# A staging pool of its own for w_out in the second product, two pairs' sums made in the first, and first w_in tiles loaded two steps sooner

## The chip, the cores and the metric

The kernel runs on one core of a Trainium2 chip. The metric is the device time of one execution in microseconds. The engines are TensorE (PE, with its weight loads as PEld), VectorE (DVE), ScalarE (ACT), GpSimd (POOL) and SyncE (SP), whose queue issues nearly all transfers.

## The reference

Attention over 8 sequences of 448 tokens with 12 heads of 64, with a sigmoid in place of the softmax, and then a feed-forward block on its 3584 x 768 output, all in float32:

```python
scores = scale * np.matmul(q, k.transpose(0, 1, 3, 2)) - np.log(S)
attn = 1.0 / (1.0 + np.exp(-scores))
x = np.matmul(attn, v) ...            # (3584, 768)
h = x @ w_in                          # (768, 2048)
relu6 = np.clip(h + 3.0, 0.0, 6.0)
g = h * relu6 / 6.0
return (g @ w_out).astype(np.float32) # (2048, 768)
```

Both weights come as float64, and the kernel turns them into float32 on the chip ("decode").

## The kernel before, in words

**Three stages.** The attention takes 168 steps of scores and attention-times-v, and 2 more. The first product (x @ w_in) is made of 7 products M1 to M7 per block (Strassen in Winograd's form), for 16 blocks q = 0 to 15, four for each of the four pairs of sequences p: 112 slots, one product of 18 matmuls in each, in the order of `slots()`. The second product (g @ w_out) has the same seven products, in the order M1, M2, M6, M7, M5, M4, M3. Five of them run over the four pairs, two units of 36 matmuls each; M6 and M3 are cut once more ("fine") and run over couples of pairs (c = 0 and 1). In all stages a float32 operand is split into a rounded part (a cast on ACT) and the rest (a subtraction on DVE), and three matmuls stand for one.

**Names.** `ws` is a w_in tile that has been loaded, `w` its split form; a slot's tile is loaded 5 slots ahead and split 3 and 2 slots ahead. `g` is the first product's output, stored to DRAM as `gd`; `gr` is such a tile read back and `gx` its split form, one for each unit of the second product (`gx_0` to `gx_7` are those of M1, `gx_8` to `gx_15` those of M2). `wo` is a raw w_out tile, decoded into `w2`; `w2s` a w_out tile read back from DRAM (`dw2`) for a product, whose split form is again `w`. `td` holds, in DRAM, the sums of g over two pairs that M6 and M3 need.

**What sets the order.** The program is written out in order for every engine, and each engine runs its own list from top to bottom. A table by slot (`at_slot`), by unit (`at_fetch`, `at_unit`, `at_end`) or by attention step (`on`, `on_late`) says at which place a piece of work is written. SP's list is one of these: a transfer that waits holds up all behind it. Each transfer also waits for the one eight places ahead of it, since eight semaphores go round.

**Staging.** Raw w_out tiles, w_in tiles and `w2s` tiles share one tag with three buffers. In the second product nine raw w_out tiles (e = 0 to 8) are loaded two units ahead of the unit in which their decode begins; one raw tile's decode is one instruction on ACT (line 66) and six on DVE (lines 68 to 79).

**Sums over two pairs.** For M6 they are made in the first product while the second of the two pairs is at work: `twin_load` reads the first pair's tile back, `twin_sums` makes four subtractions and additions of 128 x 448 on DVE, `twin_store` writes two tiles of 448 KB. For M3 they are made in the second product: `pre_load` (four loads of 448 KB), `pre_sums` (four operations of 128 x 896), `pre_store` (four stores), twice for each c; for c = 0 this starts at units 3 and 6, in M1.

The lines that set these places before:

```python
for n in range(LA):                                  # LA = 3
    on(NS - (12, 11, 8)[n], w1_load, n)
    over(on, (NS - (8, 5, 4)[n],), gen)              # cast on ACT
    over(on_late, (NS - (7, 4, 3)[n],), gen)         # rest on DVE
...
for c, n in enumerate((3, begin[M7] + 1)):
    for r in range(2):
        at_fetch(n + 3 * r, pre_load, c, r)
        at_end(n + 3 * r + 1, pre_sums)
        at_fetch(n + 3 * r + 2, pre_store, c, r)
```

Of the kernel before, what the change touches and what calls it, by code (L numbers as in the profile page):

```python
# [108 lines left out]
def tile_kernel(ctx: ExitStack, tc: tile.TileContext, qk, vP, wi, wo, outT):  # L109
# [42 lines left out]
    def staging(name, shape, dtype):  # L152
        return dw.tile(shape, dtype, tag="stg", name=name, bufs=3)
# [4 lines left out]
    def temp(tag, bufs, name, shape=(P, 2, S)):  # L158
        return tmp.tile(list(shape), F32, tag=tag, name=name, bufs=bufs)
# [9 lines left out]
    def on(s, f, *a):  # L169
        events.setdefault(s, []).append((f, a))  # L170
# [4 lines left out]
    def at_slot(n, f, *a):  # L175
        later.setdefault(n, []).append((f, a))
# [4 lines left out]
    def at_fetch(n, f, *a):  # L181
        fetch.setdefault(n, []).append((f, a))

    def at_end(n, f, *a):
        finish.setdefault(n, []).append((f, a))

    def over(when, steps, gen):
        for n in steps:
            when(n, next, gen, None)
# [104 lines left out]
            nc.sync.dma_start(out=dw1[q][:, :4, r], in_=a)  # L294
            nc.sync.dma_start(out=dw1[q][:, 4:, r], in_=s)

    def w2_unit(k, h, ec, held):

        st = staging(f"wo_{k}_{h}_{ec}", [P, FC * P, 2], I32)
        nc.sync.dma_start(out=st, in_=wo[k, h, :, ec * FC * P : (ec + 1) * FC * P])  # L300
        yield
        if ec == 0:
            held[k, h] = ring(f"w2_{k}_{h}", [P, EC, FC * P], F32)
        yield from decode(nc, st, held[k, h][:, ec])
        if ec == EC - 1 and (k, h) in ((A11, 0), (A12, 0), (A11, 1)):
# [164 lines left out]
    def twin_load(q):  # L470
        p, j = divmod(q, NQ)
        quad[q, "twin"] = temp("v", 3, f"twin_{q}")
        nc.sync.dma_start(out=quad[q, "twin"], in_=gd[p - 1, T2][:, :, j])

    def twin_sums(q):
        b1, b2 = quad[q, "twin"], quad[q, T2]
        t = quad[q, "diff"] = temp("T", 3, f"diff_{q}")
# [5 lines left out]
    def twin_store(q):
        p, j = divmod(q, NQ)
        for k, t in enumerate(("diff", "twin")):
            nc.sync.dma_start(out=td[M6, p // 2, k][:, :, j], in_=quad[q, t])
# [6 lines left out]
    def post(i, q, n):  # L493
        if i == M1:
            copied(q, "s1")
        elif i == M6:
            copied(q, "u2")
            if q // NQ % 2:
                at_slot(n + 2, twin_load, q)
        elif i == M7:  # L500
            copied(q, "u3")
            if ("D", q) in acc:
                at_slot(n + 1, c22, q, n + 1)
        elif i == M5:
# [212 lines left out]
    def w2_direct(i, h):  # L717
        w2s[i, h] = made[h].pop(WEIGHT[i])

    for e in range(3 * EC):  # L720
        k, ec = divmod(e, EC)
        gen = w2_unit((A12, A21, A22)[k], 1, ec, held)
        at_fetch(e - 2, next, gen, None)
        over(at_unit, [e, e + 1, e + 1, e + 1, e + 1], gen)
    at_unit(4, w2_keep, A12, 1)
# [27 lines left out]
        keep["up"] = stack.enter_context(tc.tile_pool(name="up", bufs=1, side="right", reuse_waits="tile"))  # L753
        return stack

    for c, n in enumerate((3, begin[M7] + 1)):
        at_fetch(n, swap, None, (), "pre", pre_open)
        for r in range(2):
            at_fetch(n + 3 * r, pre_load, c, r)
            at_end(n + 3 * r + 1, pre_sums)  # L760
            at_fetch(n + 3 * r + 2, pre_store, c, r)
        at_fetch(n + 6, swap, "pre", (), None, None)
# [201 lines left out]
```

## Time and profile before

| what | value |
|---|---|
| median of 3 runs | 1077.87 us (1077.75 to 1077.89) |
| the profiled execution's own time | 1080.59 us |
| its span, first to last instruction | 1078.8 us |
| mean granted TensorE clock, as a share of 2.4 GHz | 0.992 |
| PE busy | 1059.8 us, 98% |
| DVE busy | 808.0 us, 75% |
| ACT busy | 584.6 us, 54% |
| transfers read and written | 209.58 MB and 100.79 MB |

An engine's busy time is the sum of its instructions' time. The span leaves out 1.79 us of the profiled execution (1080.59 - 1078.8); the median of the three runs, made without a profile, is 2.72 us below that execution. A wait costs the kernel time only where it holds up PE, the engine that is busy nearly all along.

### The profile page before, as it was taken

Reading aid. Unit: us, or ns where it says so; the run is one execution under the profiler, and the core shown is the slowest. Engines: PE = TensorE matmul, PEld = TensorE weight load, DVE = VectorE, ACT = ScalarE, POOL = GpSimd, SP = SyncE. Lnnn points to the kernel's source line nnn. Section 1 sums busy time; section 2 is a strip of 40 time slices with the busy share of each in tenths; the row PEclk is TensorE's granted clock in tenths of the full one; section 3 lists DMA queues with packets and bytes.
Section 4 is the critical chain, followed back from the end, with each engine's and each line's share of the span. In section 5 each row is a group of like instructions: output and inputs, shape, how many; then the busy total and the mean of one; then the engine's idle time right before and its main releaser. Section 6 shows DMA issues by size and latency. Waiting matters only on the chain.

```text
span 1078.8 us, 16857 instructions
## 1 busy us (share of the span) xinstructions
PE 1059.8 (98%) x6728; PEld 934.0 (87%) x6728; DVE 808.0 (75%) x862; ACT 584.6 (54%) x630; POOL 41.3 (4%) x39
## 2 busy tenths in 40 slices
PE   9999999999999999999999999987999999999998
PEld 6777777776999999999999998976999999999997
DVE  3879886773578878897787777867787669787684
ACT  7889988886446644664565555333344423232441
POOL 0314230000000000000000000000000000000000
PEclk9999999999999999999999999997999999999999
DMA  8887999885867888798676898878988589899392
GB/s 320 301 310 283 380 353 331 287 298 218 283 222 224 263 315 278 275 309 304 207 232 220 294 360 305 320 284 321 338 328 286 187 322 378 328 339 348 129 395 75
DMA packets 106591, 311.50 MB, mean 289 GB/s; under 512 B 9104, under 2 KB 54416, under 8 KB 106512
## 3 DMA queue, kind: packets, MB, share of 16 engines
q1 hardware_dynamic: 106368, 310.30, 80.9%
q8 instruction: 53, 0.87, 0.3%
q14 instruction: 26, 0.21, 0.1%
q10 hardware_dynamic: 144, 0.11, 0.0%
HBM read 209.58 MB, written 100.79 MB: 288 GB/s over the span
## 4 chain that ended last, share of the span: by engine, by line
PE 93%; DMA 3%; DVE 3%; issue 0%; ACT 0%; SPq 0%; DVEq 0%; ACTq 0%
PE po L861 24%; PE A L431 21%; PE sc L221 11%; PE pv L238 11%; PE D L431 10%; PE B L431 5%; PE m_A L861 4%; PE m_E L861 4%; PE m_D L861 2%; DMA ws<-dw 1%; PE m_B L861 1%; DMA w2s<-dw 1%; DMA pre<-gd 1%; DMA gr<-gd 1%; DVE gx L87 1%
## 5 line engine op out<-in xcount | busy, mean ns | idle before, releaser
L861 PE MATMUL po<-gx,w 128*128 128x448 f32 x1440 | 294.2, 366 | 11.5 <-ACT w L85 6.9
L861 PEld LDWEIGHTS po<-gx,w 128*128 128x128 f32 x1440 | 273.7, 190 | 31.6 <-ACT w L85 7.2
L431 PE MATMUL A<-x,w 128*128 128x448 f32 x1152 | 235.8, 362 | 0.0
L431 PEld LDWEIGHTS A<-x,w 128*128 128x128 f32 x1152 | 215.9, 188 | 15.1 <-issue 0.7
L85 ACT CAST gx<-gr 128x1792 fp32r<-128x1792 f32 x68 | 115.0, 1696 | 169.1 <-PE po L861 106.0
L221 PE MATMUL sc<-qk 64*64 64x448 f32 x1344 | 189.1, 538 | 1.6 <-ACT a L223 1.6
L223 ACT ACTIVATE a<-sc,bias_s 128x896 f32<-128x896 f32 x168 | 168.3, 1011 | 37.9 <-PE sc L221 34.9
L238 PE MATMUL pv<-a,v 64*64 64x448 f32 x1344 | 188.6, 536 | 0.0
L87 DVE TENSOR_TENSOR gx<-gr,gx 128x1792 fp32r<-128x1792 f32 x68 | 137.3, 2022 | 30.6 <-ACT gx L85 30.6
L221 PEld LDWEIGHTS sc<-qk 64*64 64x64 f32 x1344 | 89.5, 134 | 39.0 <-ACT a L223 5.8
L238 PEld LDWEIGHTS pv<-a,v 64*64 64x64 f32 x1344 | 91.4, 133 | 35.0 <-issue 2.5
L431 PE MATMUL D<-x,w 128*128 128x448 f32 x576 | 120.4, 362 | 1.3 <-DVE cD L460 1.3
L87 DVE TENSOR_TENSOR w<-ws,w 128x768 fp32r<-128x768 f32 x112 | 106.3, 953 | 13.7 <-ACT w L85 12.5
L431 PEld LDWEIGHTS D<-x,w 128*128 128x128 f32 x576 | 107.9, 188 | 8.8 <-issue 1.6
L85 ACT CAST w<-ws 128x768 fp32r<-128x768 f32 x112 | 93.1, 831 | 28.6 <-DMA ws<-dw 28.5
L249 DVE TENSOR_TENSOR xr<-pv,y 128x448 f32<-128x448 f32 x48 | 29.9, 623 | 61.0 <-ACT y L248 60.8
L431 PE MATMUL B<-x,w 128*128 128x448 f32 x288 | 60.2, 362 | 0.0
L431 PEld LDWEIGHTS B<-x,w 128*128 128x128 f32 x288 | 54.0, 187 | 3.6
L451 ACT ACTIVATE g<-cD,bias 128x896 f32<-128x896 f32 x32 | 33.5, 1047 | 40.9 <-DVE cD L460 40.9
L456 ACT COPY u<-A 128x896 f32<-128x896 f32 x32 | 29.0, 907 | 48.0 <-PE A L431 48.0
L85 ACT CAST w<-w2s 128x512 fp32r<-128x512 f32 x39 | 23.1, 618 | 55.7 <-DMA w2s<-dw 33.5
L460 DVE TENSOR_TENSOR cD<-D,u 128x896 f32<-128x896 f32 x32 | 34.8, 1089 | 21.1 <-ACT u L456 13.7
(94 smaller groups left out, 945.0 us busy)
## 6 DMA issues: line engine op xcount, KB each, us to landing
gr<-gd SPq DMA_DIRECT2D x52, 896.0 KB, 6.7
ws<-dw SPq DMA_DIRECT2D x112, 384.0 KB, 4.4
gd<-g SPq DMA_DIRECT2D x64, 448.0 KB, 5.0
qk<-qk SPq DMA_DIRECT2D x47, 448.0 KB, 5.9
gd<-gT SPq DMA_DIRECT2D x32, 448.0 KB, 6.0
gr<-td SPq DMA_DIRECT2D x16, 896.0 KB, 9.0
gr<-gd SPq DMA_DIRECT2D x32, 448.0 KB, 6.3
wi<-wi SPq DMA_DIRECT2D x16, 768.0 KB, 7.9
```

Of the source, the lines that this page charges most:

```text
L85: nc.scalar.copy(hi, a)
L87: nc.vector.tensor_tensor(out=lo, in0=a, in1=hi.bitcast(F32), op=ALU.subtract)
L221: nc.tensor.matmul(out, k[halves[r], at_k], q[halves[r]], start=True, stop=True)
L223: nc.scalar.activation(a, sc[:, :, :S], AF.Sigmoid, bias=bias_s, scale=scale)
L238: nc.tensor.matmul(pv[p][halves[j], r, :S], v, a[halves[r], int(r != j) if c is None else j], start=first, stop=last)
L249: nc.vector.tensor_tensor(out=xr[b, u][:, k], in0=pv[p][:, 1, :S], in1=y, op=ALU.add)
L431: nc.tensor.matmul(t[:, j, :S], w[:, wk, j, kc], x[:, xk, kc], start=i in (M1, M2, M5) and m == 0, stop=m == 3 * KC - 1, skip_group_check= ...
L451: nc.scalar.activation(r, h, AF.Relu, bias=bias_3, scale=1.0)
L456: nc.scalar.copy(acc[key, q], acc["A", q][:, :, :S])
L460: nc.vector.tensor_tensor(out=c, in0=acc[name, q][:, :, :S], in1=acc[key, q], op=ALU.add)
L861: nc.tensor.matmul(out, w[:, wk, c], x[:, xk, c], start=first and c == 0 and xk == 0 and wk == 0, stop=last and c == FC - 1 and wk == 1, s ...
```

## The change

It has four parts.

1. The first three w_in tiles are loaded 2, 2 and 1 attention steps sooner, and their splits are made 1, 0 and 1 steps later.
2. `w2_unit` takes the function that gives it a staging buffer. In the second product the tiles e = 3 to 8 get theirs from a pool `wo` of their own with three buffers, open from unit 1 to 5 units ahead of M6. The tiles e = 0 to 2 keep the shared tag.
3. M3's sums for c = 0 (the first two pairs) are made in the first product, with `twin_load`, `twin_sums` and `twin_store`, at 5, 8 and 10 slots after M3 of the blocks q = 7 to 10. Their `pre_load`, `pre_sums` and `pre_store` in the second product are gone. For this case both tiles are read back, the second into a buffer of tag `T` (`mate`).
4. The M6 sums of block q = 14 are made 4 slots later.

```diff
-    def w2_unit(k, h, ec, held):
+    def w2_unit(k, h, ec, held, stage=staging):
...
-        st = staging(f"wo_{k}_{h}_{ec}", [P, FC * P, 2], I32)
+        st = stage(f"wo_{k}_{h}_{ec}", [P, FC * P, 2], I32)
...
-        on(NS - (12, 11, 8)[n], w1_load, n)
+        on(NS - (14, 13, 9)[n], w1_load, n)
         gen = w1_split(n)
-        over(on, (NS - (8, 5, 4)[n],), gen)
-        over(on_late, (NS - (7, 4, 3)[n],), gen)
+        over(on, (NS - (7, 5, 3)[n],), gen)
+        over(on_late, (NS - (6, 4, 2)[n],), gen)
...
+    def twin_load(i, c, j, k, mate=None):
+        b1 = temp("v", 3, f"twin_{i}_{c}_{j}")
+        nc.sync.dma_start(out=b1, in_=gd[2 * c, k][:, :, j])
+        if mate is None:
+            mate = temp("T", 3, f"mate_{i}_{c}_{j}")
+            nc.sync.dma_start(out=mate, in_=gd[2 * c + 1, k][:, :, j])
...
             if q // NQ % 2:
-                at_slot(n + 3, twin_sums, q)
-                at_slot(n + 5, twin_store, q)
+                twin, held_up = (M6, q // NQ // 2, q % NQ), 4 * (q == NPR * NQ - 2)
+                at_slot(n + 3 + held_up, twin_sums, *twin, (q, T2))
+                at_slot(n + 5 + held_up, twin_store, *twin)
+            if 0 <= q - 2 * NQ + 1 < NQ:
+                twin = M3, 0, q - 2 * NQ + 1
+                at_slot(n + 5, twin_load, *twin, B22)
+                at_slot(n + 8, twin_sums, *twin)
+                at_slot(n + 10, twin_store, *twin)
...
+    at_fetch(1, w2_open)
+    at_fetch(begin[M6] - 5, w2_pool.close)
...
-        gen = w2_unit((A12, A21, A22)[k], 1, ec, held)
+        gen = w2_unit((A12, A21, A22)[k], 1, ec, held, staging if e < 3 else w2_stage)
...
-    for c, n in enumerate((3, begin[M7] + 1)):
...
+    n = begin[M7] + 1
```

**SP's list at the end of the attention**, before. `qk` and `v` are the attention's last inputs, `ws_0` to `ws_2` the first w_in tiles, `dw2` the stores of decoded w_out tiles.

```order
L198 DMA qk_46_2562<-qk 128x896
L203 DMA v_46_2564<-vP 128x896
L198 DMA qk_47_2610<-qk 128x896
L335 DMA dw2_4_0_79<-w2S1_0_2339 128x1536
L335 DMA dw2_5_0_81<-w2_0_0_2274 128x1536
L352 DMA ws_0_2637<-dw1_0_69 128x768
L352 DMA ws_1_2653<-dw1_0_69 128x768
L313 DMA dw2_1_0_75<-w2_1_0_2463 128x1536
L352 DMA ws_2_2695<-dw1_0_69 128x768
```

The same place in the change:

```order
L198 DMA qk_46_2562<-qk 128x896
L203 DMA v_46_2564<-vP 128x896
L352 DMA ws_0_2604<-dw1_0_69 128x768
L198 DMA qk_47_2612<-qk 128x896
L352 DMA ws_1_2621<-dw1_0_69 128x768
L335 DMA dw2_4_0_79<-w2S1_0_2339 128x1536
L335 DMA dw2_5_0_81<-w2_0_0_2274 128x1536
L352 DMA ws_2_2677<-dw1_0_69 128x768
L313 DMA dw2_1_0_75<-w2_1_0_2463 128x1536
```

The first two tiles now stand ahead of the two stores, and the third ahead of one.

**DVE's list where the first product ends**, before. `gx_0` to `gx_2` are the splits of the second product's first units, the `diff` and `twin` rows are M6's sums of blocks 14 and 15, `cD_15` is the sum for which the last M3 product waits, `gT` the last sums of `g`.

```order
L87 TENSOR_TENSOR gx_0_6047<-gr_0_5990,gx_0_6047 128x1792 [waits DMAHW1_49,Activation_49]
L478 TENSOR_TENSOR diff_14_6086<-gT2_14_6051 128x448 [waits DMAHW5_49,DVE_49]
L479 TENSOR_TENSOR diff_14_6086<-gT2_14_6051,twin_14_5872 128x448
L480 TENSOR_TENSOR twin_14_5872<-diff_14_6086,twin_14_5872 128x448 [waits DVE_49]
L481 TENSOR_TENSOR twin_14_5872<-twin_14_5872 128x448 [waits DVE_49]
L442 SCALAR_TENSOR_TENSOR g0_15_6074<-g0_15_6074,cB_15_6072 128x896 [waits Activation_49]
L460 TENSOR_TENSOR cD_15_6111<-D_15_6092,u3_15_6042 128x896 [waits PE_49]
```

The same list in the change, from `gx_1` on. Its rows from `gx_0` to `cD_15` read as before without the four rows of block 14.

```order
L87 TENSOR_TENSOR gx_1_6216<-gr_1_6127,gx_1_6216 128x1792 [waits DMAHW6_49,Activation_49]
L442 SCALAR_TENSOR_TENSOR g7_15_6199<-g7_15_6199,cD_15_6197 128x896 [waits DMAHW2_49,DVE_49]
L484 TENSOR_TENSOR diff_5_1_2_6221<-gT2_14_6095 128x448 [waits DMAHW5_49]
L485 TENSOR_TENSOR diff_5_1_2_6221<-gT2_14_6095,twin_5_1_2_5916 128x448
L486 TENSOR_TENSOR twin_5_1_2_5916<-diff_5_1_2_6221,twin_5_1_2_5916 128x448 [waits DVE_49]
L487 TENSOR_TENSOR twin_5_1_2_5916<-twin_5_1_2_5916 128x448 [waits DVE_49]
L465 TENSOR_TENSOR gT3_15_6227<-g2_15_6152,g7_15_6199 128x896 [waits DMAHW0_49,DVE_49]
L467 TENSOR_TENSOR gT2_15_6229<-gT3_15_6227,g0_15_6118 128x896 [waits DMAHW1_49,DVE_49]
L87 TENSOR_TENSOR gx_2_6237<-gr_2_6211,gx_2_6237 128x1792 [waits DMAHW5_49,Activation_49]
L484 TENSOR_TENSOR diff_5_1_3_6281<-gT2_15_6229 128x448 [waits DMAHW4_49,DVE_49]
```

Block 14's four rows have moved from ahead of `cD_15` to ahead of `gT3_15`. The `diff` of block 15 (last row) is written into the buffer of block 14's, so it waits (DMAHW4) for the store of that one to land.

**SP's list in M1 of the second product**, before. `w2s_1_0` and `w2s_1_1` are M2's two weight tiles, `wo_3_1_*` the last raw w_out tiles.

```order
L300 DMA wo_3_1_1_6477<-wo 128x1024 [waits DMAHW0_49,DVE_49]
L669 DMA td_2_0_0_115<-pre_0_0_2_6366 128x896 [waits DMAHW1_49]
L669 DMA td_2_0_0_115<-pre_0_0_7_6364 128x896 [waits DMAHW2_49]
L669 DMA td_2_0_1_116<-pre_0_0_0_6360 128x896 [waits DMAHW3_49]
L669 DMA td_2_0_1_116<-pre_0_0_1_6362 128x896 [waits DMAHW4_49]
L597 DMA w2s_1_0_6483<-dw2_1_0_75 128x1536 [waits DMAHW5_49,DVE_49]
L575 DMA gr_9_6485<-gd_0_1_88 128x1792 [waits DMAHW6_49,Activation_49]
L300 DMA wo_3_1_2_6535<-wo 128x1024 [waits DMAHW7_49,DVE_49]
L656 DMA pre_0_1_0_6537<-gd_0_2_89 128x896 [waits DMAHW1_49,DMAHW0_49]
```

The same place in the change:

```order
L300 DMA wo_3_1_1_6509<-wo 128x1024 [waits DMAHW4_49,DVE_49]
L609 DMA w2s_1_0_6511<-dw2_1_0_75 128x1536 [waits DMAHW5_49]
L587 DMA gr_9_6513<-gd_0_1_88 128x1792 [waits DMAHW6_49,Activation_49]
L300 DMA wo_3_1_2_6563<-wo 128x1024 [waits DMAHW7_49,DVE_49]
L587 DMA gr_10_6565<-gd_1_1_94 128x1792 [waits DMAHW0_49,Activation_49]
L609 DMA w2s_1_1_6622<-dw2_1_1_76 128x1536 [waits DMAHW3_49,DMAHW1_49]
```

The `pre` loads and `td` stores are gone from between, and `w2s_1_0` and `w2s_1_1` no longer wait for DVE.

## Rows read from the trace of the kernel before

**Rows 1.** The page, part 1: busy time, share of the span, instructions.

```profile
PE 1059.8 (98%) x6728; PEld 934.0 (87%) x6728; DVE 808.0 (75%) x862; ACT 584.6 (54%) x630; POOL 41.3 (4%) x39
```

**Rows 2.** Stretches: length, busy PE PEld DVE ACT POOL, clock, DMA share, GB/s.

```profile
259.30:650.00 390.70, 390.70 (x1958) 366.28 (x1955) 304.06 (x307) 215.50 (x246) 0.00 (x0) 1.00 0.80 266
...
721.00:730.00 9.00, 4.41 (x14) 3.30 (x13) 6.16 (x9) 5.40 (x6) 0.00 (x0) 0.73 0.13 52
730.00:743.40 13.40, 6.61 (x29) 5.75 (x27) 7.34 (x7) 0.59 (x2) 0.00 (x0) 0.75 0.91 340
743.40:755.00 11.60, 11.52 (x45) 10.38 (x46) 11.20 (x17) 7.40 (x8) 0.00 (x0) 0.76 0.91 353
```

**Rows 3.** Timeline of PE, 640 to 860 us: start, length, what [idle before].

```profile
660.40 3.85 PE L431 MATMUL D<-x,w 128*128 128x448 f32 x18 [1.27 <-DVE cD L460]
664.09 57.77 PE L861 MATMUL po<-gx,w 128*128 128x448 f32 x288
724.98 0.60 PE L861 MATMUL po<-gx,w 128*128 128x448 f32 x1 [3.12 <-ACT gx L85]
727.04 9.57 PE L861 MATMUL po<-gx,w 128*128 128x448 f32 x35 [1.46 <-DVE gx L87]
743.48 53.27 PE L861 MATMUL po<-gx,w 128*128 128x448 f32 x252 [6.87 <-ACT w L85]
796.59 2.56 PE L861 MATMUL m_A<-gx,w 128*128 128x448 f32 x12
```

**Rows 4.** The chain that ended last, 840 to 1030 us: start, length, what.

```profile
849.55 172.80 PE po L861 x864
```

**Rows 5.** Timeline of all engines, 640 to 750 us, around M2's first weights.

```profile
701.96 1.09 DVE L660 TENSOR_TENSOR pre<-pre,pre 128x896 f32<-128x896 f32 x1 [2.77 <-DMA pre<-gd]
...
709.91 0.33 SPq L300 DMA_DIRECT2D wo<-wo  x1
710.29 3.45 SPq L669 DMA_DIRECT2D td<-pre  x4
...
715.28 0.32 SPq L597 DMA_DIRECT2D w2s<-dw  x1
...
722.20 1.14 ACT L85 CAST w<-w2s 128x512 fp32r<-128x512 f32 x2 [12.84 <-DMA w2s<-dw]
...
742.81 1.66 ACT L85 CAST w<-w2s 128x512 fp32r<-128x512 f32 x3 [15.21 <-DMA w2s<-dw]
```

**Rows 6.** Timeline of all engines where the attention ends, 222 to 275 us.

```profile
238.29 1.66 SPq L352 DMA_DIRECT2D ws<-dw  x2
...
248.28 0.83 ACT L85 CAST w<-ws 128x768 fp32r<-128x768 f32 x1 [2.44 <-DMA ws<-dw]
...
250.07 0.98 PE L221 MATMUL sc<-qk 64*64 64x448 f32 x8 [1.59 <-ACT a L223]
```

**Rows 7.** Timeline of DVE where the first product ends, 655 to 684 us.

```profile
655.77 0.62 DVE L478 TENSOR_TENSOR diff<-gT 128x448 f32<-128x448 f32 x1
...
658.17 1.08 DVE L442 SCALAR_TENSOR_TENSOR g<-g,cB 128x896 f32<-128x896 f32 x1
...
675.21 0.62 DVE L478 TENSOR_TENSOR diff<-gT 128x448 f32<-128x448 f32 x1
...
681.04 2.02 DVE L87 TENSOR_TENSOR gx<-gr,gx 128x1792 fp32r<-128x1792 f32 x1
```

**Rows 8.** Transfers issued at 676.3, 478.5 to 480.5 and 484.4: KB, us to landing.

```profile
td<-diff SPq DMA_DIRECT2D x1, 448.0 KB, 6.2
...
gd<-gT SPq DMA_DIRECT2D x2, 448.0 KB, 8.9
...
ws<-dw SPq DMA_DIRECT2D x1, 384.0 KB, 9.5
```

**Rows 9.** Timelines of SP and of DVE near slot 67 of the first product.

```profile
484.45 1.26 SPq L352 DMA_DIRECT2D ws<-dw  x1
...
502.03 1.82 DVE L87 TENSOR_TENSOR w<-ws,w 128x768 fp32r<-128x768 f32 x2
```

More of the change, by code (lines that the diff above doesn't have):

```diff
@@ L468, in g_sums, with twin_sums @@
         quad[q, T3], quad[q, T2] = t3, t2
[L470 to L477, printed above, removed]
+    twins = {}
+    def twin_load(i, c, j, k, mate=None):
[4 more added lines that the diff above has]
+            nc.sync.dma_start(out=mate, in_=gd[2 * c + 1, k][:, :, j])
+        twins[i, c, j] = b1, mate
+    def twin_sums(i, c, j, mate=None):
+        b1, b2 = twins[i, c, j]
+        b2 = quad[mate] if mate else b2
+        t = temp("T", 3, f"diff_{i}_{c}_{j}")
         nc.vector.tensor_tensor(out=t[:, 1], in0=b2[:, 1], in1=b2[:, 0], op=ALU.subtract)
@@ L481, in twin_sums, with twin_store @@
         nc.vector.tensor_tensor(out=b1[:, 1], in0=b1[:, 1], in1=b1[:, 0], op=ALU.subtract)
[L483 to L486, printed above, removed]
+        twins[i, c, j] = t, b1
+    def twin_store(i, c, j):
+        for k, t in enumerate(twins.pop((i, c, j))):
+            nc.sync.dma_start(out=td[i, c, k][:, :, j], in_=t)
     def c22(q, n):
@@ L498, in post @@
             if q // NQ % 2:
-                at_slot(n + 2, twin_load, q)
+                at_slot(n + 2, twin_load, M6, q // NQ // 2, q % NQ, T2, ())
         elif i == M7:
@@ L718, in w2_direct, with w2_open, w2_stage @@
         w2s[i, h] = made[h].pop(WEIGHT[i])
+    keep, w2_pool = {}, ExitStack()
+    def w2_open():
+        keep["wo"] = w2_pool.enter_context(tc.tile_pool(name="wo", bufs=3, side="right", reuse_waits="tile"))
+    def w2_stage(name, shape, dtype):
+        return keep["wo"].tile(shape, dtype, tag="wo", name=name)
+    at_fetch(1, w2_open)
+    at_fetch(begin[M6] - 5, w2_pool.close)
     for e in range(3 * EC):
         k, ec = divmod(e, EC)
-        gen = w2_unit((A12, A21, A22)[k], 1, ec, held)
+        gen = w2_unit((A12, A21, A22)[k], 1, ec, held, staging if e < 3 else w2_stage)
         at_fetch(e - 2, next, gen, None)
@@ L754, in up_open @@
         return stack
-    for c, n in enumerate((3, begin[M7] + 1)):
[L757 to L762, printed above, removed]
+    n = begin[M7] + 1
+    at_fetch(n, swap, None, (), "pre", pre_open)
+    for r in range(2):
+        at_fetch(n + 3 * r, pre_load, 1, r)
+        at_end(n + 3 * r + 1, pre_sums)
+        at_fetch(n + 3 * r + 2, pre_store, 1, r)
+    at_fetch(n + 6, swap, "pre", (), None, None)
     for i in TWICE:
@@ L802, in tile_kernel @@
     xt_ctx[B22].close()
-    keep, po, so, banks = {}, {}, {}, {}
+    po, so, banks = {}, {}, {}
     SIXTH = 1.0 / 6.0
```

## The prediction

> **What bounds the kernel now.** The page comes first: PE is busy for 1059.8 of 1078.8 us [rows 1]. At most about 19 us of the span can be idle PE, so the question is where PE waits, and what runs slowly. The stretches show it next. The first product is solid: PE is busy for all of 390.70 us at full clock [rows 2]. Just behind it, from 721 to 755 us, PE idles and the granted clock falls to about three quarters of 2.4 GHz, a mean of stretches at 2.4 and at 1.2 [rows 2]. PE's timeline gives the gaps: 3.12, 1.46 and 6.87 us around M2's first two units, and 1.27 us ahead of the first product's last slot [rows 3]. A fifth gap, 1.59 us, lies where the attention ends [rows 6]. In the undisturbed chain 864 matmuls take 172.80 us [rows 4], so one is 0.200 us, a unit of 36 is 7.2 us and a slot of 18 is 3.6 us.
>
> What the middle costs follows from that. M1 and M2 are 576 matmuls, 115.2 us; they take 796.59 - 664.09 = 132.5 us [rows 3]. So 17.3 us are lost: 11.45 us idle, and 5.85 us by matmuls at the lower clock (35 in 9.57 us instead of 7.0, and more behind 743.48) [rows 3].
>
> Why PE waits there is read backwards. ACT stood 12.84 us and later 15.21 us for M2's weight tiles `w2s` [rows 5]. The first of these was issued at 715.28, behind four `td` stores and a raw `wo` tile at 709.91 [rows 5]; that tile waited for a buffer that DVE's decode frees. DVE was late because it had stood until 701.96 for the `pre` loads and then made four sums of 1.09 us each [rows 5]. So one chain runs through the shared staging tag and the `pre` work: loads, sums, decode, buffer, `w2s`, cast.
>
> **The change, part by part.** Times below are on the clock of the old trace; each gain moves all that follows.
>
> *First w_in tiles.* Both old tiles were issued at 238.29, and the first cast waited 2.44 us for its tile, at 248.28; the next score matmuls started 1.59 us late [rows 6]. The first tile now stands ahead of a `qk` load and two stores, and its cast is one step later. The old tile took 10 us (238.29 to 248.28); issued about 3 us sooner, it lands near 245.3, some 2 us ahead of the later cast. Gain between 0 (a later gap takes its place) and 1.59; I take 1.6, since both margins point one way. The two stores slip by two issues; nothing reads them for hundreds of microseconds.
>
> *Block 14's sums.* Their four operations took DVE from 655.77 to 658.17, 2.40 us [rows 7], ahead of the sum for which PE waited 1.27 us [rows 3]. With 2.40 us less ahead of it, the sum is ready before PE: gain 1.27.
>
> They now lie ahead of `gT3_15`. DVE is 1.27 us earlier there and then 2.40 us later, so `gx_3`, which ended at 683.06 [rows 7], ends at 684.19. Unit 3 is due at 664.09 + 21.6 - 1.27 = 684.42. That leaves 0.2 us. Next in line is the new wait: block 15's `diff` (at 675.21 [rows 7], now 676.34) needs the store of block 14's `diff`, issued at about 671.2, after `g7_15` and the second of the four operations. At 6.2 us to landing [rows 8] that is 677.4, 1.1 us late; at 9.5 us it is 680.7, 4.4 us late. Against that, two stores of 448 KB have left the crowded queue ahead of it, so a landing of 5 to 6 us is nearest. I take 0.5 us of PE time, between 0 and 4.
>
> *The pool for `wo` and the sums taken out of M1.* DVE loses 8 x 1.09 us of `pre` sums and the stand ahead of them, SP 16 transfers. Tiles e = 3 to 5 wait for no buffer, and `w2s_1_0` for no decode. It still stands behind `wo` e = 7, which waits for the decode of e = 4. DVE's list from `gx_3` on is decode, split, decode, split: 3.4 us for a decode (from the end of the sums, 675.21 + 2.40, to 681.04) and 2.0 for a split [rows 7]. So `gx_6` ends at 684.2 + 3 x 5.4 = 700.4 and the decode of e = 4 at 703.8. Issue 704, landing by 713.5 at 9.5 us [rows 8], cast by 714.5; M2 is due at 664.09 - 1.27 + 57.6 = 720.4. The margin is 6 us, so M2's start costs nothing. The second tile is issued behind e = 8, near 710, and lands by 719.5 for a unit due at 727.6. With no gap there, the clock has no reason to fall. Gain 17.3, at least 11.45 if the clock fell for another reason.
>
> The Trainium skill (TensorE: Matmul & The Clock Gate, section "HAM oscillation — how this bites in real kernels") prices throttled time at half its length. The three stretches hold 4.9 + 6.7 + 5.6 = 17.1 us below full clock (twice the missing share of each) [rows 2], which that rule makes 8.6 us, and the middle 20.0 instead of 17.3. The row count of matmuls decides for me: PE idled through part of the slow time, which costs nothing twice.
>
> *The sums put into the first product.* Each of four blocks gets two loads and two stores of 448 KB and four operations, 2.40 us of DVE [rows 7]. DVE is busy for 304.06 of 390.70 us there [rows 2], so 9.6 us more fit on average; a place has to be checked. The worst is the first, near slot 67. The two loads come in at about 484.4, ahead of the w_in tile that was issued at 484.45 [rows 9]. The second takes a buffer of tag `T` and waits for a `gT` store that lands 8.9 us behind its issue [rows 8], so SP stops there for 3 to 5 us. The tile itself landed in 9.5 us [rows 8], in a full queue; 896 KB more ahead of it are 2.7 us at 340 GB/s [rows 2], which pass while SP stands. So it is 2.7 to 5 us late, and DVE 5 to 7.4 us late with the sums. The split for slot 69 ended at about 503.0 (first of two at 502.03 [rows 9]); slot 69 starts at 259.3 + 69 x 3.6 = 507.7. The slack of 4.7 us is used up: PE waits for 0.3 to 2.7 us if all goes that way, and not at all if the tile had some slack itself. I take 0.5. At the other three blocks the queue is shorter; 2.4 us against the same kind of slack costs nothing.
>
> On this the Trainium skill (DMA: Bandwidth & Descriptors, section "Queues, rings and completion order") says that completions need not come in the order of issue. By that rule the tile could land as if alone and the 0.5 would be 0; no row here is needed for it.
>
> **Sum.** 1.6 + 1.27 + 17.3 - 0.5 - 0.5 = 19.2 us off the profiled span: 1078.8 to 1059.6, and with the 1.79 us around it 1061.4. The median of the runs lies 2.72 below the profiled execution; if that carries over in full the time is 1077.87 - 19.2 = 1058.7, and if the 2.72 were made of the same gaps, 1061.4. I take **1058.7 us**; its own range is 1056.8 to 1061.4.
>
> **The rivals.** *A new wait in M1* (chance 0.20). ACT's first `s` of M1 now also waits for the store of block 15's `twin`, whose buffer it takes over, and all casts stand behind it. If both stores take 9.5 us: `gx_3` is 4.2 us late, that store is issued at 683.1 and lands at 692.6, and with some 6 us behind it (an estimate: DVE's split of 2.02 us [rows 7], ACT's work of about twice that) `gx_4` ends near 698.6, due at 691.6 + 4.2 = 695.8: 2.8 us more. With up to 2.6 us at half clock behind such a gap (as behind 727.04 [rows 3]) it costs up to 9.5 us: 1060.5 to 1067.5. For it: the queue there is full. Against: it lost two stores.
>
> *Slots 67 to 70 pile up* (0.08): 1.5 to 3 us of PE in place of 0.5, 1059.7 to 1061.2.
>
> *M2 still starts late* (0.05): the decode chain is DVE's, and if M1's casts are late as above the margin of 6 us goes and a gap like 6.87 us with its slow clock returns, 7 to 14 us: 1066 to 1073.
>
> *No gain* (0.02): the sums were never on the path, and DVE is late for another reason. The 2.77 us wait at 701.96 [rows 5] speaks against it.
>
> *Slower* (0.03): the stop of SP at the `mate` load. Every later w_in tile stands behind it, in four blocks. It decides once four such stops cost 20.2 + 2.2 us of PE, 5.6 each: with 4.7 us of slack less 2.4 of sums that is a tile 8 us late, four times, where I count 2.7 to 5 once. Then the time is 1080 or more.
>
> **Chances.** My forecast has 0.62. The range of 1056.3 to 1065.5 holds it, the pile-up and about two thirds of the first rival. About 0.2% (2 us) is what a measurement of this kernel can tell from no change; faster by more than that 0.95, within it 0.02, slower 0.03.
>
> **What would show it.** Right: no idle time of PE ahead of the scores near 250 us and ahead of the last slot; PE solid from M1's start to M6 at full clock; ACT's casts of `w2s` without a wait of over 10 us. Wrong: `diff` waiting for `td` by several microseconds, then PE waiting for `gx_3` or `gx_4`; PE idle near slot 69; a granted clock below 1 anywhere behind 20 us. The prediction fails as a whole if PE still waits at M2's first unit, or if w_in tiles come late in all four blocks.

## The result and the profile after

The changed kernel takes 1063.59 us (median of 4 runs, 1061.90 to 1064.67) against 1077.88 before; the ratio is 0.9866, 95% interval 0.9849 to 0.9883. That is 14.3 us faster. It lies in the forecast's range, but 4.9 us above the point of 1058.7 and outside the likeliest case's own range of 1056.8 to 1061.4. The profiled execution took 1064.27 us, its span is 1062.4 us. A second set of four runs gave 1062.74 us (1061.75 to 1065.63).

The page of the change, part 1:

```profile
PE 1055.1 (99%) x6728; PEld 925.2 (87%) x6728; DVE 809.0 (76%) x870; ACT 585.3 (55%) x630; POOL 41.3 (4%) x39
```

PE idles for some 7 us of the span now, where it was 19 [rows 1]. The stretches of [rows 2], and two new ones (length, busy PE PEld DVE ACT POOL, clock, DMA share, GB/s):

```profile
259.30:650.00 390.70, 390.70 (x1955) 366.21 (x1955) 313.18 (x322) 216.85 (x245) 0.00 (x0) 1.00 0.84 284
721.00:730.00 9.00, 9.00 (x46) 8.44 (x45) 8.79 (x14) 5.10 (x6) 0.00 (x0) 1.00 0.49 170
730.00:743.40 13.40, 13.40 (x68) 12.56 (x67) 12.79 (x12) 3.40 (x2) 0.00 (x0) 1.00 0.60 206
743.40:755.00 11.60, 11.60 (x60) 10.87 (x58) 9.35 (x6) 3.39 (x2) 0.00 (x0) 1.00 0.93 349
682.70:685.29 2.59, 0.00 (x1) 0.00 (x0) 2.59 (x3) 2.02 (x3) 0.00 (x0) 1.00 0.97 352
685.29:690.00 4.71, 4.71 (x16) 4.27 (x17) 4.54 (x7) 3.68 (x3) 0.00 (x0) 0.64 0.97 373
```

From 721 to 755 us, where PE idled and the clock fell before, PE is solid at full clock. In their place stands one new gap of 2.59 us in M1, with 4.71 us at a granted clock of 0.64 behind it. PE's timeline at the old gaps (start, length, what, idle before):

```profile
254.94 2.55 PE L238 MATMUL pv<-a,v 64*64 64x448 f32 x24
257.42 3.88 PE L431 MATMUL A<-x,w 128*128 128x448 f32 x18
...
657.13 3.76 PE L431 MATMUL D<-x,w 128*128 128x448 f32 x18
660.73 21.97 PE L883 MATMUL po<-gx,w 128*128 128x448 f32 x109
685.29 95.27 PE L883 MATMUL po<-gx,w 128*128 128x448 f32 x467 [2.59 <-DVE gx L87]
780.40 2.56 PE L883 MATMUL m_A<-gx,w 128*128 128x448 f32 x12
```

The waits at the end of the attention, at the last slot and in M2 [rows 3, 6] are gone. M1 and M2 take 780.40 - 660.73 = 119.67 us where they took 132.5; undisturbed it would be 115.2. So 4.47 us are still lost there, all in M1: 2.59 idle and 1.88 more. Some 0.27 of the 1.88 belongs to the stop itself: where PE stopped and the clock stayed at full, the stretch also grew by more than the idle time shown (before, the last slot: 404.84 - 403.31 - 1.27 = 0.26; M1 in e11 below: 117.33 - 115.20 - 1.85 = 0.28). The other 1.6 us go to the slower clock.

What M1 waits for is in the chain that ended last, followed through that stretch (start, length, what):

```profile
667.74 0.54 DVE diff L484
668.28 0.55 DVE diff L485
...
668.85 8.45 DMA td<-diff
...
677.38 0.63 DVE diff L484
...
683.22 2.03 DVE gx L87
```

and in the timelines of DVE and of ACT:

```profile
677.38 0.63 DVE L484 TENSOR_TENSOR diff<-gT 128x448 f32<-128x448 f32 x1 [3.18 <-DMA td<-diff]
...
683.27 1.29 ACT L845 ACTIVATE s<-po 128x1344 f32<-128x1344 f32 x1 [13.40 <-DMA td<-twin]
```

Block 14's `diff` is stored at 668.85 and lands 8.45 us later. Block 15's `diff`, at 677.38, is written into the same buffer and had waited 3.18 us for it. Behind it DVE makes the sums and a decode, and only then the rest of `gx_3`, which ends at 685.25, 2.5 us after unit 2 was through (660.73 + 21.97 = 682.70).

**Theories.** W: that wait for the landing of the store makes the gap and its slow clock. A: ACT's stand of 13.40 us for the store of a `twin`, also new, makes M1 late. B: the 2.40 us of sums moved behind the last slot have no room there, wait or no wait. For M2: S, the shared staging buffers kept its weights late; P, the `pre` work alone did.

### The profile page after: what moved, and what is told of

Same layout as the page of the kernel before. It is cut to its first block, busy times and chain, and to the rows that moved or that the text cites. A ratio compares the mean times of both kernels' runs of the same rounds, so it can differ in the third digit from the quotient of the medians.

```text
span 1062.4 us, 16868 instructions
## 1 busy us (share of the span) xinstructions
PE 1055.1 (99%) x6728; PEld 925.2 (87%) x6728; DVE 809.0 (76%) x870; ACT 585.3 (55%) x630; POOL 41.3 (4%) x39
## 4 chain that ended last, share of the span: by engine, by line
PE 97%; DMA 1%; DVE 1%; issue 0%; ACT 0%; SPq 0%; DVEq 0%
PE po L883 25%; PE A L431 22%; PE pv L238 12%; PE sc L221 12%; PE D L431 11%; PE B L431 5%; PE m_A L883 4%; PE m_E L883 4%; PE m_D L883 2%; PE m_B L883 1%; DMA td<-diff 1%; DMA v<-vP 0%; DVE gx L87 0%; ACT gx L85 0%; DVE diff L484 0%
## 5 line engine op out<-in xcount | busy, mean ns | idle before, releaser
L883 PE MATMUL po<-gx,w 128*128 128x448 f32 x1440 | 290.2, 363 | 2.6 <-DVE gx L87 2.6
L238 PE MATMUL pv<-a,v 64*64 64x448 f32 x1344 | 184.8, 536 | 0.3 <-DMA v<-vP 0.3
L221 PE MATMUL sc<-qk 64*64 64x448 f32 x1344 | 184.9, 536 | 0.0
```

Of the source, the lines that this page charges most:

```text
L221: nc.tensor.matmul(out, k[halves[r], at_k], q[halves[r]], start=True, stop=True)
L238: nc.tensor.matmul(pv[p][halves[j], r, :S], v, a[halves[r], int(r != j) if c is None else j], start=first, stop=last)
L883: nc.tensor.matmul(out, w[:, wk, c], x[:, xk, c], start=first and c == 0 and xk == 0 and wk == 0, stop=last and c == FC - 1 and wk == 1, s ...
```

## The experiments

Time by stretch, from PE's timelines of each profile, in us. The stretches start at the first attention-times-v matmul, the first product's first matmul, M1's and M6's first; "rest" is from M6 to the end of the span. Each ratio is to runs of the kernel before made beside it (medians 1077.75 to 1078.47). Most kernels have four runs; e5 has ten, e7 six, e12 five.

| kernel | first matmul | attention | first product | M1 and M2 | rest | median of runs | ratio to before, interval |
|---|---|---|---|---|---|---|---|
| before | 6.78 | 252.47 | 404.84 | 132.50 | 282.2 | 1077.88 | 1 |
| change | 6.68 | 250.74 | 403.31 | 119.67 | 282.0 | 1063.59 | 0.9866 (0.9849 to 0.9883) |
| e1 block 14's sums back | 7.26 | 250.40 | 404.83 | 115.20 | 282.0 | 1061.81 | 0.9847 (0.9831 to 0.9862) |
| e2 its diff in another buffer | 7.33 | 250.40 | 403.59 | 115.20 | 282.1 | 1060.28 | 0.9831 (0.9815 to 0.9846) |
| e3 pool alone | 7.64 | 251.29 | 404.82 | 121.05 | 282.0 | 1068.40 | 0.9905 (0.9889 to 0.9920) |
| e4 sums moved, alone | 7.82 | 251.64 | 404.83 | 116.91 | 282.0 | 1064.88 | 0.9873 (0.9854 to 0.9892) |
| e5 w_in tiles alone | 7.82 | 250.41 | 404.84 | 129.79 | 282.3 | 1078.08 | 0.9998 (0.9989 to 1.0007) |
| e6 block 14's sums 2 slots later | 6.92 | 250.72 | 405.15 | 115.31 | 282.1 | 1061.30 | 0.9842 (0.9828 to 0.9857) |
| e7 block 14's sums 4 later, alone | 7.08 | 252.49 | 403.32 | 135.41 | 282.1 | 1082.14 | 1.0036 (1.0021 to 1.0051) |
| e8 e2, first of M3's sums five times | 7.75 | 250.41 | 411.31 | 115.19 | 282.0 | 1066.43 | 0.9891 (0.9873 to 0.9909) |
| e9 e2 without the w_in part | 7.37 | 251.69 | 403.31 | 115.20 | 282.0 | 1061.86 | 0.9847 (0.9832 to 0.9861) |
| e10 e2 without the pool | 7.33 | 250.57 | 403.31 | 120.52 | 282.1 | 1065.03 | 0.9870 (0.9854 to 0.9887) |
| e11 the change again | 6.49 | 250.53 | 404.24 | 117.33 | 282.0 | 1062.74 | 0.9859 (0.9842 to 0.9876) |
| e12 e2, M3's sums a slot later | 7.15 | 250.74 | 404.22 | 115.20 | 282.1 | 1061.15 | 0.9835 (0.9821 to 0.9848) |

### e1, block 14's sums back

```diff
-                twin, held_up = (M6, q // NQ // 2, q % NQ), 4 * (q == NPR * NQ - 2)
+                twin, held_up = (M6, q // NQ // 2, q % NQ), 0
```

> The change with block 14's sums put back to their old place (ahead of the sum that the last slot waits for). Theory W (the 2.59 us gap in M1 comes from block 15's diff waiting for the store of block 14's diff): that store is then issued about 10 us sooner, diff does not wait, M1 and M2 take 115.2 us in place of 119.67, and PE waits again about 1.27 us ahead of the first product's last slot. Span 1062.4 - 4.47 + 1.27 = 1059.2, time about 1060.5. Rival A (ACT's stand of 13.40 us for a td store makes M1 late, whichever block's sums come first): a gap of 2 us or more stays in M1, span about 1063.5, time about 1065.

PE's timeline:

```profile
658.81 3.85 PE L431 MATMUL D<-x,w 128*128 128x448 f32 x18 [1.27 <-DVE cD L460]
662.49 115.36 PE L883 MATMUL po<-gx,w 128*128 128x448 f32 x576
```

As W had it: the 1.27 us are back, M1 and M2 run without a gap in 115.2 us. The time, 1061.81, is 1.3 above the 1060.5 expected; the span of 1059.7 is 0.5 above. In the profiles the fourth part cost more than it brought: 4.47 us in M1 against 1.53 in the first product (404.84 to 403.31). The runs lean the same way but overlap: 1061.58 to 1063.05 here, 1061.75 to 1065.63 in the eight of the change.

### e2, block 14's diff in a buffer of another tag

```diff
-        t = temp("T", 3, f"diff_{i}_{c}_{j}")
+        tag = ("a", 4) if (i, c, j) == (M6, 1, 2) else ("T", 3)
+        t = temp(*tag, f"diff_{i}_{c}_{j}")
```

> The change with block 14's diff in a buffer of another tag (a, four buffers, idle by then), all else in place. Theory W: diff of block 15 no longer waits 3.18 us, gx_3 ends about 682.1 against a due time of 682.3, no gap, no slow clock; M1 and M2 take 115.2 to 115.7 us, span 1057.9 to 1058.4, time 1058.5 to 1060, and the runs lie within 1 us of each other, since no store's landing is on the path. Rival B (the sums' own 2.40 us of DVE behind the first product are what M1 has no room for): a gap of 1 to 3 us stays and the span is 1060 or more. Rival A (ACT's stand for the td store): gx_4 late instead, span 1060 to 1062.

DVE's and PE's timelines, ACT's at the stand that theory A speaks of, and the store issued at 669.43 (KB, us to landing):

```profile
674.71 0.62 DVE L485 TENSOR_TENSOR diff<-gT 128x448 f32<-128x448 f32 x1
...
680.54 2.02 DVE L87 TENSOR_TENSOR gx<-gr,gx 128x1792 fp32r<-128x1792 f32 x1
```

```profile
661.32 115.36 PE L884 MATMUL po<-gx,w 128*128 128x448 f32 x576
```

```profile
683.89 1.30 ACT L846 ACTIVATE s<-po 128x1344 f32<-128x1344 f32 x1 [13.42 <-DMA td<-twin]
```

```profile
td<-diff SPq DMA_DIRECT2D x1, 448.0 KB, 8.6
```

The sums stand where the change put them, the 2.40 us are there, and ACT still stands 13.42 us for the `twin` store. Block 14's store takes as long as in the change (8.6 us, to 678.0, against 8.4), but `diff` of block 15 starts at 674.71 without a wait. Only that wait is gone, and with it the gap and the slow clock. `gx_3` ends at 682.56, due at 661.32 + 21.6 = 682.92. That settles W against A and B. The runs are 1059.96 to 1060.79, every one below all eight runs of the change (1061.75 to 1065.63): with the landing off the path most of the scatter went too. By its median this is the fastest version here, 17.6 us below the 1077.88 of before.

### e3, the pool alone

The kernel before, with the pool's functions and

```diff
-        gen = w2_unit((A12, A21, A22)[k], 1, ec, held)
+        gen = w2_unit((A12, A21, A22)[k], 1, ec, held, staging if e < 3 else w2_stage)
```

> The kernel before with the pool for w_out alone; the pre loads, sums and stores stay in M1. Theory S (the shared staging buffers tie M2's weights to DVE's decode): w2s_1_0 is issued right behind the four td stores, near 711.5 in place of 715.28, and w2s_1_1 near 718 in place of 733.59. The gaps at 724.98 and 727.04 shrink to 0 to 2 us and that at 743.48 goes: 12 to 17 us gained, time 1061 to 1066. Rival P (the pre work on DVE and SP is what makes M2 late): less than 8 us gained, time above 1070.

PE's timeline, SP's, and SP's of the kernel before at the second tile:

```profile
722.14 7.28 PE L871 MATMUL po<-gx,w 128*128 128x448 f32 x35 [0.43 <-DVE gx L87]
731.46 0.67 PE L871 MATMUL po<-gx,w 128*128 128x448 f32 x2 [2.04 <-ACT w L85]
733.10 51.86 PE L871 MATMUL po<-gx,w 128*128 128x448 f32 x250 [0.98 <-DVE w L87]
```

```profile
710.42 1.13 SPq L597 DMA_DIRECT2D w2s<-dw  x1
...
717.28 0.32 SPq L597 DMA_DIRECT2D w2s<-dw  x1
```

```profile
733.59 0.38 SPq L597 DMA_DIRECT2D w2s<-dw  x1
```

The tiles are issued at 710.42 and 717.28, as S had it, 4.9 and 16.3 us sooner than 715.28 [rows 5] and 733.59. M1 and M2 gain 11.45 us. The time of 1068.4 lies between S's range (up to 1066) and P's (above 1070), so neither cause is the whole: a wait of 2.04 + 0.98 us stays at the second unit, with the clock at 0.75 of full in the 4.54 us from 731.46 and at 0.89 in the 5 us after that.

### e4, the sums moved, alone

The change with its first, second and fourth parts taken back; of these the pool:

```diff
-    at_fetch(1, w2_open)
-    at_fetch(begin[M6] - 5, w2_pool.close)
...
-        gen = w2_unit((A12, A21, A22)[k], 1, ec, held, staging if e < 3 else w2_stage)
+        gen = w2_unit((A12, A21, A22)[k], 1, ec, held)
```

> The kernel before with M3's sums for the first two pairs made in the first product, and nothing else of the change; w_out and w2s share the staging buffers as before. Theory S: w2s_1_0 is issued near 709 and in time, but w2s_1_1 still waits for the decode of e = 7, near 720, lands near 730 for a unit due at 729: a gap of 1 to 4 us with a slow clock behind it, time 1064 to 1068. Rival P (the pre work alone is what made M2 late): no gap in M2, time 1060.5 to 1062. If the first product has no room for the sums, gaps near slots 67 to 90 of it show, which the run with everything did not show.

```profile
664.29 64.97 PE L881 MATMUL po<-gx,w 128*128 128x448 f32 x324
730.37 51.00 PE L881 MATMUL po<-gx,w 128*128 128x448 f32 x252 [1.11 <-ACT w L85]
```

S again: the first tile in time, the second cast late, a gap of 1.11 us on PE. The `pre` work was the larger cause: without it M1 and M2 gain 15.6 us, with the pool alone 11.45. The two gains overlap, as both lie on one chain.

### e5, the w_in tiles alone

```diff
-        on(NS - (12, 11, 8)[n], w1_load, n)
+        on(NS - (14, 13, 9)[n], w1_load, n)
```

(and the splits as in the change; the rest is the kernel before)

> The kernel before with the first part alone (the first three w_in tiles 2, 2 and 1 attention steps sooner, their splits 1, 0 and 1 steps later). Theory F (the first cast waits for its tile): no idle PE ahead of the scores near 250 us, the first product starts 0.9 to 2.0 us sooner (the gap cost 1.97 us in the profile of before, 0.89 and 1.24 us in those of the pool alone and of the sums alone), and all of it is kept: time 1076 to 1077. Rival: M2's weight tiles arrive at times set by the transfers, so part of the gain goes into longer waits at M2's first units: time 1077.5 to 1078.5.

No idle PE near 250 us, and the attention's stretch is 2.06 us shorter. But the time is that of before: 1078.08 in ten runs against 1078.24 in fifteen, interval -1.2 to +0.8 us. By that interval a gain of over 1.2 us is excluded. In the profile M2 still waits 1.34, 1.59 and 7.75 us:

```profile
722.18 0.47 PE L861 MATMUL po<-gx,w 128*128 128x448 f32 x1 [1.34 <-ACT gx L85]
724.24 8.68 PE L861 MATMUL po<-gx,w 128*128 128x448 f32 x35 [1.59 <-DVE gx L87]
740.67 52.36 PE L861 MATMUL po<-gx,w 128*128 128x448 f32 x252 [7.75 <-ACT w L85]
```

The result speaks for the rival, but this profile (1077.02 us, the fastest of its ten) has the gain still in it. What takes the place of it in the others is not shown. The test with M2 free of waits is e9.

### e6, block 14's sums 2 slots later

```diff
-                twin, held_up = (M6, q // NQ // 2, q % NQ), 4 * (q == NPR * NQ - 2)
+                twin, held_up = (M6, q // NQ // 2, q % NQ), 2 * (q == NPR * NQ - 2)
```

> The change with block 14's sums 2 slots later than before in place of 4, where DVE stood idle for 1.11 and 1.47 us. Theory W: the store of its diff is issued near 660 and lands before block 15's diff asks for the buffer near 674.5; the sum that the last slot waits for stands ahead of them. No idle PE at the last slot and none in M1, and gx_1 ends 0.8 us later than in the change, 0.4 us before it is due. M1 and M2 take 115.2 us, time 1058.5 to 1060.5, as with a buffer of its own. Rival B (the sums have no room anywhere at the end of the first product): gx_1 or gx_2 late, a gap of 0.5 to 2 us at M1's second unit and a slow clock behind it, time 1061 to 1064.

```profile
662.79 115.48 PE L883 MATMUL po<-gx,w 128*128 128x448 f32 x576 [0.78 <-DVE g L442]
```

No wait for the store, none at the last slot, but 0.78 us at M1's very first matmul, in a place that neither theory named. (The table counts it in the first product, which also lost 0.8 us further up, 0.22 of them idle at 600.53.) PE waits there for DVE's `g` of M4, which reads a bank of PSUM and stood behind the sums (661.65 in place of 658.37 in the change). The time of 1061.3 is 0.8 above W's range.

### e7, block 14's sums 4 slots later, alone

The kernel before, with

```diff
-                at_slot(n + 3, twin_sums, q)
-                at_slot(n + 5, twin_store, q)
+                held_up = 4 * (q == NPR * NQ - 2)
+                at_slot(n + 3 + held_up, twin_sums, q)
+                at_slot(n + 5 + held_up, twin_store, q)
```

> The kernel before with the fourth part alone (block 14's sums 4 slots later). Theory W: the 1.27 us ahead of the last slot are gone and a gap of 1 to 4 us comes up in M1 near 683 us behind block 15's diff; as M2's first weights come late at a time that transfers and DVE set, M1's gap is partly hidden in the waits that follow: time 1076 to 1079. Rival G (the fourth part does what it does in the sum of the forecast, 1.27 us gained and at most 0.5 lost): no gap in M1, time 1076.5 to 1077.1.

```profile
686.55 36.09 PE L862 MATMUL po<-gx,w 128*128 128x448 f32 x179 [1.69 <-DVE gx L87]
727.77 0.74 PE L862 MATMUL po<-gx,w 128*128 128x448 f32 x1 [5.13 <-ACT gx L85]
...
746.24 52.22 PE L862 MATMUL po<-gx,w 128*128 128x448 f32 x252 [6.32 <-ACT w L85]
```

The gap in M1 came (1.69 us), so G falls. But it was not hidden in M2's waits, as I had expected: the first of these grew from 3.12 [rows 3] to 5.13 us. M2's weights hang on DVE's list, and DVE's stand before `diff`, 2.28 us here, pushes that list: the first `w2s` was issued at 718.73, 3.45 us later than the 715.28 of before. The fourth part alone makes the kernel 0.36% slower.

### e8, the cost of M3's sums doubled

```diff
+        for _ in range(5 if i == M3 else 1):
             nc.vector.tensor_tensor(out=t[:, 1], in0=b2[:, 1], in1=b2[:, 0], op=ALU.subtract)
```

> The change with block 14's diff in a buffer of its own, and with the first of M3's four sums made five times in place of once in each of the four blocks (the same numbers again, 2.2 to 2.5 us more of DVE): the suspected cost of the sums in the first product doubled. In the change the splits of the w_in tiles ended 1.4 us before the start of slot 69, 1.9 before 83, 2.1 before 89, 2.3 before 68 and 2.7 or more before the others near these sums (before: 4.7 at the nearest). Theory D (the tile's split is behind the sums on DVE, and nothing else gives room): PE waits 0.8 to 1.1 us at slot 69, 0.3 to 0.6 at 83 and 0 to 0.4 at 89, in all 1 to 2.5 us, time 1061.5 to 1063. Rival (the splits wait for their tiles and not for DVE): no idle PE in the first product, time as without the repeated sums, 1060.3.

(The 4.7 us quoted there for before are those of slot 69; the nearest of all was 3.2, at slot 56.) PE's timeline:

```profile
501.56 12.66 PE L431 MATMUL A<-x,w 128*128 128x448 f32 x54 [1.92 <-ACT u L456]
558.27 3.88 PE L431 MATMUL A<-x,w 128*128 128x448 f32 x18 [0.46 <-DVE w L87]
562.74 3.48 PE L431 MATMUL A<-x,w 128*128 128x448 f32 x16 [0.58 <-DVE w L87]
585.85 7.08 PE L431 MATMUL A<-x,w 128*128 128x448 f32 x34 [1.14 <-DVE w L87]
608.15 11.07 PE L431 MATMUL A<-x,w 128*128 128x448 f32 x54 [0.81 <-ACT u L456]
```

The three gaps that wait for DVE's `w`, 2.18 us in all, are of D's kind and within its 1 to 2.5. The other two are of a kind that D did not name: PE waits for ACT's copy `u`, which stood behind casts that had waited for their tiles, for 0.81 us at the last and for 1.92 us at the first. There the repeated sums begin at 498.54, and the cast for which ACT's copy `u` stood back waited for its tile until 499.87. SP had stopped for 4.4 us at the `mate` load in this execution (2.8 in the change's profile). In all, the first product takes 7.7 us longer than in e2, 4.9 of them idle. This execution is the slowest of the four runs (1068.53; the others 1065.20 to 1067.38).

### e9, e10, e11: parts left out of e2, and the change again

e9 has the old steps of the w_in tiles (12, 11, 8), e10 the staging buffers in place of the pool; both keep the rest of e2. e11 is the change.

> The change with block 14's diff in a buffer of its own, and without the first part (the first three w_in tiles and their splits where they were before). Theory F (the first part's gain was there in the kernel with that part alone and was lost again in M2's waits, which took 132 us however early M1 began): with M2 free of waits the gain is seen, 0.9 to 2.0 us, so this kernel takes 1061.2 to 1062.3, with 0.7 to 1.6 us of idle PE ahead of the scores near 250 us. Rival (the first part gains nothing anywhere): 1060.0 to 1060.6, as with that part.

> The change with block 14's diff in a buffer of its own, and without the pool: w_out's raw tiles and w2s share the staging buffers as before. Theory S (w2s_1_1 waits for the decode of e = 7): the second w2s tile is cast about 8 us later than the 721.47 of the kernel with the pool, and PE stands 1 to 2.5 us at M2's second unit, as it stood 1.11 us in the kernel with the sums alone; M1 and M2 take 116.5 to 119 us, time 1061.7 to 1064. Rival P (with the sums gone the shared buffers cost nothing): 115.2 us, 1060.3.

> The change itself, once more, beside the others on the same chip. Theory W (its scatter comes from the landing of one store that DVE waits for): a gap of 1 to 4 us in M1 near 683 us again, times spread over 2 to 3 us between 1062 and 1065, while the kernel with a buffer of its own spread over 0.8 us. Rival: the gap is absent and the time is near 1060.5, so that the first profile showed a chance event.

PE's timeline of e9, of e10 and of e11:

```profile
249.88 0.98 PE L221 MATMUL sc<-qk 64*64 64x448 f32 x8 [0.81 <-ACT a L223]
...
662.37 115.36 PE L884 MATMUL po<-gx,w 128*128 128x448 f32 x576
```

```profile
661.21 64.97 PE L882 MATMUL po<-gx,w 128*128 128x448 f32 x324
729.61 52.28 PE L882 MATMUL po<-gx,w 128*128 128x448 f32 x252 [3.43 <-ACT w L85]
```

```profile
499.14 11.07 PE L431 MATMUL A<-x,w 128*128 128x448 f32 x54 [0.64 <-ACT u L456]
...
685.08 93.68 PE L883 MATMUL po<-gx,w 128*128 128x448 f32 x467 [1.85 <-DVE gx L87]
```

e9: the wait near 250 us is back, the attention's stretch is 1.29 us longer than e2's, and the median 1.6 us above it (not the same runs of before). So the first part pays once M2 waits for nothing, as F had it. e10: S in kind, but more than its 116.5 to 119 us: a gap of 3.43 us and 120.52 us, and a time 1.0 above its range. Block 14's sums now stand in M1's list, ahead of the decode that the second tile waits for: it is issued 60.75 us after M1's start, in e4 58.52. e11: the gap of M1 again (1.85 us, DVE waiting 2.44 us for the store, which landed after 7.7 us), and 0.64 us at slot 67, which the first profile did not have.

### e12, M3's sums a slot later

```diff
-                at_slot(n + 5, twin_load, *twin, B22)
-                at_slot(n + 8, twin_sums, *twin)
-                at_slot(n + 10, twin_store, *twin)
+                at_slot(n + 6, twin_load, *twin, B22)
+                at_slot(n + 9, twin_sums, *twin)
+                at_slot(n + 11, twin_store, *twin)
```

> The change with block 14's diff in a buffer of its own, and with M3's sums for the first two pairs one slot later throughout (loads 6, sums 9, stores 11 slots after the block's M3, in place of 5, 8 and 10). Theory Q (SP's stop at the mate load, 2.9 us in the change and 4.5 us where the repeated sums ran, puts the w_in tiles behind it close to their slots): the store that the load waits for has landed by then, SP stops for less than 1 us, the split nearest to its slot ends 2.5 us or more ahead of it in place of 1.0 to 1.7, and the time is 1059.5 to 1060.5 with runs within 0.8 us. Rival (the loads' bytes make the tiles late, wherever they stand): some split still ends 1 to 2 us ahead of its slot, time 1060 to 1061.5.

Q falls. SP stops for only 0.6 us at the `mate` load, but by 3.6 us a slot splits still end 0.5 us ahead of their slots (83 and 90), and PE waits 0.17 and 0.18 us for ACT's `u` elsewhere. The time is 1061.15, no better than e2. That leaves the loads' bytes and DVE's own 2.40 us per block as candidates; which of them it is was not tried.

## Why the range held and the likeliest value did not

**The sum against the profile.** Forecast span 1059.6, measured 1062.4, 2.8 more. By the table above the attention gave 1.73 for the 1.6 forecast, the first product 1.53 for 0.77 (1.27 less 0.5), M1 and M2 12.83 for 16.8 (17.3 less 0.5); start and rest gave another 0.3. The one bad term is M1's. (The 1.53 are the 1.27 of the last slot and the 0.26 that its stop cost beyond the idle time; the 0.5 for slot 69 was not needed in this execution.)

**The step that failed** is "I take 0.5 us of PE time, between 0 and 4" for `diff` of block 15. The mechanism was named, and so was the outcome at a long landing. I took a landing of 5 to 6 us from the 6.2 of the store at 676.39 [rows 8], since two stores had left the queue. It was 8.4. The transfers issued from 665 to 674 us (KB each, us to landing):

```profile
gr<-gd SPq DMA_DIRECT2D x1, 896.0 KB, 8.3
gd<-gT SPq DMA_DIRECT2D x2, 448.0 KB, 8.4
gd<-g SPq DMA_DIRECT2D x1, 448.0 KB, 8.4
td<-diff SPq DMA_DIRECT2D x1, 448.0 KB, 8.4
td<-twin SPq DMA_DIRECT2D x1, 448.0 KB, 8.2
```

The moved store was issued 1 and 2 us behind loads and stores of 448 and 896 KB. The row I used was issued 2.5 us behind the last of the same burst, when more of it had been worked off. Rows for the new place were at hand: the burst's own landings, 7.9 to 8.1 us for the transfers issued from 670 to 674 us before. By the prediction's own formula 8.4 us make `diff` 3.3 us late, and 3.18 were measured, so the formula held and its landing time did not. The gap of 2.59 us also brought 1.88 us beyond the idle time, most of it by the slower clock, of which the 0.5 had nothing: the 4.47 us lie outside the "between 0 and 4" too. So the rival "a new wait in M1" (0.20, 1060.5 to 1067.5) came true by its first half, and with it two signs of being wrong: `diff` waiting for `td`, and a granted clock below 1. Its second half did not: ACT's first `s` stood 13.40 us for the `twin` store, and in e2 13.42, and no unit was late by it. The forecast's range held because it took in two thirds of that rival, not because its likeliest case came about.

**The median.** The second error is 2.0 us: I carried over in full that the median lay 2.72 us below the profiled execution. In the change it lies 0.68 below. My other reading, that the 2.72 were made of the same gaps, was nearer; in e2, where those gaps are gone, the median lies 0.14 below.

**What held.** *M2's weights*: forecast issue 704 and cast by 714.5, then a second issue near 710; measured 705.23, a cast that began at 713.66, and 711.13. (The forecast's times are on the old trace's clock; M1 began at 660.73 where it had 664.09 - 1.27.) The whole 17.3 us came back where `diff` does not wait (115.20 us in e1, e2, e9 and e12). (Of the 5.85 us in it that the prediction gave to the lower clock, some 0.8, an estimate, are what the three stops cost beyond their idle time, 0.27 each.) The Trainium skill (TensorE: Matmul & The Clock Gate, section "HAM oscillation — how this bites in real kernels") prices throttled time at half its length. By the prediction's estimate from that rule the gain would have been 20.0; the runs decide for 17.3. For the new slow stretch, where PE was busy all along, the same rule gives an estimate of 1.7 us (4.71 us at 0.64), which agrees with the 1.6 measured.

*The last slot*: its wait of 1.27 us is gone, as forecast, and the first product is 1.53 shorter; e1 gives both back. *The splits*: `gx_3` without the wait ends 0.36 us ahead of its unit in e2, forecast 0.2. *Slot 69*: SP stopped 2.8 us at `mate` (forecast 3 to 5), and the split ended 1.42 us ahead of its slot where it had 4.7, so 3.3 us were used up (forecast 5 to 7.4). PE waited for nothing there in the change's profile and 0.64 us at slot 67 in e11. In the eight profiles with these sums in this place the first product lost nothing in five, 0.3 us in e2, 0.8 in e6 and 0.9 in e11, so 0.5 was of the right size. "At the other three blocks it costs nothing" held by 1.9 us (slot 83). *The w_in tiles*: 1.6 forecast, 1.73 in the profile, 1.3 between e9 and e2.

*Slower*, the stop of SP in all four blocks, stayed far off: even with the sums' time doubled and a stop of 4.4 us (e8) the kernel lost 6 us to e2, where that rival needed 22. *Slots 67 to 70 pile up* needed 1.5 to 3 us; the most seen there without repeated sums is e11's 0.9. *M2 still late* and *no gain* did not occur.

## What to carry to other kernels

When work is moved later, look up the reuse of every buffer it holds until its store lands, and take the landing time from transfers issued in the same burst, at the new place. A stand of an engine that works through a tight list is paid by everything behind it; it is not hidden in a later wait that the same list feeds. Each part alone can be worth nothing or less than nothing (e5, e7) while the same part pays when the rest is in place (e2 takes 1.6 us less than e9, which lacks the first part, and 1.5 less than e1, which lacks the fourth and the buffer of its own), so parts are tried by leaving one out of the whole as well as by adding one.

## What the runs showed of the hardware that was not expected

The granted clock did not fall behind every gap (a share between 0.5 and 1 is a mean of time at 1.2 and at 2.4 GHz). Behind a gap of 2.59 us it was 0.64 for 4.7 us, behind 3.43 us (e10) 0.61 for 4.4, behind 1.92 us (e8) 0.62 for 4.4. Behind 2.04 and 0.98 us (e3) it was 0.65 for 4.9. It stayed at 1.00 behind 1.85 us and 0.64 us (e11), 1.69 us (e7), 1.27 us (before) and 1.11 us (e4). For e11 (the clock is the third number from the right):

```profile
685.08:690.00 4.92, 4.92 (x25) 4.61 (x26) 4.75 (x7) 3.69 (x3) 0.00 (x0) 1.00 0.98 379
```

These are single executions; no run set the length of a gap on purpose, so they give no limit.

The same store of 448 KB landed after 3.3 us once the queue had run almost empty (at 678.57 in the change) and after 8.4 in the burst, whose landings came in the order of issue (at 675.1, 676.2, 677.3 and 678.4). And the first attention-times-v matmul, which waits for the first transfers, began anywhere between 6.49 and 7.82 us, so 1.3 us of the differences between single executions come from their start alone.
